# Order of matmuls in an attention-plus-MLP kernel: three constants of the order's planner against a table with one entry per group

## The chip, the cores and the metric

The kernel runs on one core of a Trainium2 chip. The metric is the time on the device of one execution, in microseconds (us); the median of several runs is given. Every detail of where the time goes comes from one execution that the hardware profiler recorded.

## The reference

Two steps in a row. The first is an attention with 32 inducing points over 4 batches of 12480 tokens of 128 channels; the second is an MLP of width 2048 with a leaky activation whose slope is a parameter.

```python
def mab(q, kv):
    s = scale * (q @ kv.transpose(0, 2, 1))
    s = s - s.max(-1, keepdims=True)
    a = np.exp(s)
    a /= a.sum(-1, keepdims=True) + 1e-09
    return a @ kv
h = mab(I, x)                 # x (4, 12480, 128), I: 32 inducing points per batch
attn = mab(x, h)              # (4, 12480, 128)

x = attn.reshape(49920, 128)
h = x @ w_in                  # (49920, 2048)
g = np.maximum(h, 0.0) + alpha * np.minimum(h, 0.0)
return g @ w_out              # (49920, 128), float32
```

## The kernel before

**The algebra.** The activation is written as alpha*h + (1 - alpha)*relu(h). The linear part is folded into one 128x128 matrix per batch. Since the attention's output for a token is a weighted mean of only 32 rows, the product with w_in is folded too: for each batch the 32 rows are multiplied by w_in once (`hW`), and a token's row of 2048 follows from its 32 weights, so this matmul contracts over 32 and takes only 32 of the array's 128 rows.

**The work of a group.** Tokens are taken in groups of 512 (the last one of a batch is smaller: 192). There are 25 groups per batch, 100 in all. For each group the kernel does

- 16 *fills* (`fill`): a matmul of 32 rows, `bank<-rep,hW`, which makes one chunk of 128 hidden channels for 512 tokens in a PSUM bank; ScalarE (ACT) or VectorE (DVE) takes it out of the bank through a relu into an SBUF tile `gt` (L608 and L611). The planner gives each to the engine that it expects to be done first.
- 16 x 4 *pieces* (`piece`): each chunk is contracted over its 128 channels with W1, in four matmuls of 32 rows each, `bank<-gt,W`, one on each of the array's four row tiles, all added up in the group's own accumulator bank.
- one *linear* term, `bank<-rep,hA`, which opens the accumulator.
- at the end (`finish`) a transpose on DVE (L658), a multiplication on GpSimd (POOL, L661) and four stores that POOL issues (L675).

There are 8 PSUM banks. The accumulators of groups in work and the banks between fill and relu share them.

**Lanes.** 92 of the 100 groups are *laned*; the others (two first, the small ones, two last) are done with full-array matmuls. A laned group starts on row tile 0 and does its 16 pieces there, moves to row tile 1 and does its 16 pieces there, and so on to row tile 3. So up to `LANES` = 4 groups are in work at once, one per row tile, and matmuls on different row tiles run side by side. At each move there is a fence: the pieces on the next row tile wait for the last one on the tile before. Fills can go to any row tile; one on a tile that has a lane takes a turn from that lane's pieces. At most `KEPT` - 1 = 65 chunks are kept in SBUF.

**What sets the order.** `tokens` builds the program once, ahead of the run. It keeps a planner's clock for each engine (`clk.pe`, `clk.act`, `clk.dve`, and for each bank the time it comes free) and in a loop writes the next matmul: it collects the candidates with the time at which each could go and a rank, and takes the earliest, by rank among equals. Candidates are pieces, lane entries, the start of a new group on row tile 0, and fills. PE, ACT and DVE run what was written in that order. Three choices in that loop matter here:

- *When a fill is due.* `hungry = min(clk.act, clk.dve) < clk.pe + HUNGRY` with `HUNGRY` = 600 (ns): when the engine that takes out relus and is done first has less than 600 ns of planned work ahead, a fill may go to any row tile and ranks ahead of a piece; otherwise it may go only to an empty row tile and ranks last.
- *When a new group may start.* `if f == 0 and queue and sum(map(bool, tile)) + len(moving) < LANES`: as soon as row tile 0 is free and fewer than four groups are in work.
- *Which row tile a fill takes.* Among equal times an empty one first (rank 0.5 against 0.6).

At the start of each laned group `run_tasks` also writes the work of that moment for attention: scores, exponentials, denominators, the loads of the next batch and its transposes. These hang on the number of the group, so their order against the groups is fixed, while their place among the matmuls follows the groups' starts.

Of the kernel before, what the change touches and what calls it, by code (L numbers as in the profile page):

```python
# [2 lines left out]

# [17 lines left out]
SUP = GRP * NQ  # L21
NBANK = 8
LANES = 4
HUNGRY = 600
TAIL = 2
AHEAD = 8
LAND = 8000
# [3 lines left out]
XTS = 8  # L31
DONE = 420
SWITCH = 110


@with_exitstack
def kernel(
# [23 lines left out]
    KC = DFF // P  # L61
# [47 lines left out]
    clk = Clock()  # L109
    idle = list(range(NBANK - 2))  # L110

    def bank():
        i = min(idle, key=lambda i: clk.free[i])
        idle.remove(i)
        clk.pe = max(clk.pe, clk.free[i])
        return banks[i]
# [12 lines left out]
    def mm(o, lhsT, rhs, start=True, stop=True, **kw):  # L129
        return pin(nc.tensor.matmul(o, lhsT, rhs, start=start, stop=stop, **kw))  # L130
# [454 lines left out]
    def spent(b, g, n):  # L585
        left[b, g] -= n
        if not left[b, g]:
            held.append((b, g))
# [26 lines left out]
    def piece(ch, i, rows=slice(0, P)):  # L615
        b, g, u = ch
        pp, nb, cp = shape_of(g)
        t = pp * nb
        return add(b, g, W1[rows, u * cp + i, :], seen[ch][0][rows, i * t : (i + 1) * t])

    def whole(ch):
        clk.pe = max(clk.pe, seen[ch][1])
        for i in range(shape_of(ch[1])[2]):
            piece(ch, i)
        clk.pe += 217
        spent(ch[0], ch[1], 4)
        seen.pop(ch)

    def linear(b, g, f):
        st = states[b]  # L630
        pp, nb, _ = shape_of(g)
        rows = slice(32 * f, 32 * f + 32)
        add(b, g, st.hA[rows, :], st.rep[g][rows, : pp * nb])
        spent(b, g, 1)

    def linear_whole(b, g):
        st = states[b]
        pp, nb, _ = shape_of(g)
        add(b, g, st.hAq[:], st.rep[g][:, : pp * nb])
        clk.pe += 217  # L640
        spent(b, g, 1)

    def flush():
        while held:
            finish(*held.pop(0))
# [166 lines left out]
    def tokens(st):  # L812
# [7 lines left out]
        laned = [y for y in every if y not in direct]  # L820
        first = {y: m for m, y in enumerate(laned)}
        wholes = [[] for _ in laned]
        for b in range(B - 1):
            c = first[b + 1, 0] - 1
# [28 lines left out]
        for b in range(B):  # L853
            base = T0 + (first[b, 0] if b else -2)
            for s in range(1, NS + 1):
                t = base + 4 * s - AHEAD if b or s > 2 else 4 * s - 2
# [48 lines left out]
        def run_tasks(t):  # L905
            for fn in tasks.pop(t, []):
                fn()
# [22 lines left out]

        clk.pe += SWITCH
        fence = ctx.enter_context(nc.semaphore())
        fenced = 0
        fences = {}
        queue = list(laned)
        tile = [None] * 4
        moving = []
        free_at = [clk.pe] * 4
        gate = {}
        closed = False  # L940
        fresh = {f: bank() for f in (2, 3)}

        def pause(t):
            return t in pauses or (t - T0 < len(wholes) and wholes[t - T0])

        def fillable():
            if not need or len(seen) >= KEPT - 1:
                return False
            b, g, _ = need[0]
            return b in states and g in states[b].rep and hasattr(states[b], "hW")  # L950

        while queue or moving or any(tile):
            best = []
            taken = {q for _, q, _ in moving}
            for f in range(4):
                if tile[f]:
                    y, todo = tile[f]
                    if todo[0] is None:
                        best.append((free_at[f], 0, f, "linear"))
                    elif (*y, todo[0]) in seen:  # L960
                        t = max(free_at[f], seen[*y, todo[0]][1] - 100)
                        best.append((t, 1, f, "piece"))
                else:
                    for y, q, t in moving:
                        if q == f:
                            best.append((max(free_at[f], t), 1, f, "enter"))
                    if f == 0 and queue and sum(map(bool, tile)) + len(moving) < LANES:
                        ch = (*queue[0], 0)
                        if ch in seen:
                            t = max(free_at[f], seen[ch][1] - 100 - SLOT)  # L970
                            best.append((t, 2, f, "start"))
            if fillable():
                since = max(min(clk.free[i] for i in idle) - 40, landed.get(need[0][:2], 0))
                hungry = min(clk.act, clk.dve) < clk.pe + HUNGRY
                for f in range(4):
                    t = max(free_at[f], since)
                    if hungry:
                        best.append((t, 0.5 + 0.1 * bool(tile[f]), f, "fill"))
                    elif not tile[f]:
                        best.append((t, 4 + (f in taken), f, "fill"))  # L980
            soon = min(max(x[0], clk.pe) for x in best) < clk.pe + 2 * SLOT
            for f in sorted(fresh):
                if soon and f not in taken:
                    best.append((free_at[f], 9, f, "warm"))
            assert best, (need[:2], len(seen), tile, moving, queue[:2])
            if closed:
                calm = [x for x in best if x[3] == "piece" and x[2] and x[2] not in gate]
                calm += [x for x in best if x[3] == "warm"]
                best = calm or [x for x in best if x[3] == "piece"] or best
            t, _, f, what = min(best, key=lambda x: (max(x[0], clk.pe), x[1]))  # L990
            closed = False
            clk.pe = max(clk.pe, t)
            rows = slice(32 * f, 32 * f + 32)
            if what == "start":
                m = first[queue[0]]
                if pause(T0 + m):
                    clk.pe = max(clk.pe, max(free_at) + SWITCH)
                    for ch in wholes[m]:
                        if ch[:2] not in begun:
                            linear_whole(*ch[:2])  # L1000
                        whole(ch)
                    flush()
                    run_tasks(T0 + m)
                    clk.pe += SWITCH
                    free_at = [clk.pe] * 4
                else:
                    run_tasks(T0 + m)
                tile[0] = [queue.pop(0), [None] + list(range(KC))]
                continue
            if what == "enter":  # L1010
                x = next(x for x in moving if x[1] == f)
                moving.remove(x)
                tile[f] = [x[0], list(range(KC))]
                gate[f] = fences[x[0], f]
                if f in fresh:
                    i = number[id(fresh.pop(f))]
                    clk.free[i] = clk.pe + SLOT
                    idle.append(i)
                continue
            if what == "warm":  # L1020
                mm(
                    fresh[f][:], W1[rows, 0, :],
                    W1[rows, 0:NB, :].rearrange("p k c -> p (k c)"), skip_group_check=True,
                )
                free_at[f] = clk.pe + SLOT
                continue
            if what == "fill":
                fill(need.pop(0), f)
            else:
                y, todo = tile[f]  # L1030
                u = todo.pop(0)
                if u is None:
                    linear(*y, f)
                else:
                    ch = (*y, u)
                    m = piece(ch, 0, rows)
                    if f in gate:
                        m._wait_ge(fence, gate.pop(f))
                    spent(*y, 1)
                    if f == 3:  # L1040
                        seen.pop(ch)
                    if not todo:
                        tile[f] = None
                        if f < 3:
                            pin(nc.tensor.drain(fusable=True)).then_inc(fence, 1)
                            fenced += 1
                            closed = True
                            fences[y, f + 1] = fenced
                            moving.append((y, f + 1, clk.pe + DONE))
                        flush()  # L1050
            free_at[f] = clk.pe + SLOT
        clk.pe = max(clk.pe, max(free_at) + SWITCH)
        for t in sorted(tasks):
# [12 lines left out]
        assert not tasks and not seen and not any(left.values()), (tasks, seen, left)  # L1066

    tokens(st)


# [28 lines left out]
```

## Time and profile before

| | us |
|---|---|
| median of 3 runs | 571.53 |
| lowest and highest | 570.17, 576.52 |
| the profiled execution | 570.76 |
| its span, first to last instruction | 569.0 |

| engine | busy us | share of the span |
|---|---|---|
| PE (matmuls) | 551.0 | 97% |
| DVE | 500.3 | 88% |
| ACT | 510.4 | 90% |
| POOL | 408.5 | 72% |

Busy time is the union of an engine's records, so two matmuls side by side on different row tiles count once, and records of ACT or DVE that overlap by their pipeline count once. A row of the list of groups names the line of the kernel, engine and operation, the tiles written and read, the shape, the count, and then busy us, mean ns of one, and the idle time before them with what ended it. L130 is the line of the helper that records nearly all matmuls, so those are told apart by their tiles: `gt,W` are pieces, `rep,hW` fills, `rep,hA` linear terms, `W` alone are dummy matmuls on lanes that are still empty at the beginning.

The mean granted clock of TensorE over the span is 0.992.

### The profile page before, as it was taken

What the parts mean: (1) busy time and instruction counts of PE and PEld (TensorE: products, weight loads), DVE (VectorE), ACT (ScalarE), POOL (GpSimd) and SP (SyncE); (2) the same over time, 40 slices, a digit from 0 to 9 for tenths busy, and PEclk for the clock granted to TensorE, in tenths of its full rate; (3) what the DMA queues carried; (4) which work ended last, traced back from release to release, by engine and by line L of the source; (5) the groups of instructions that cost most, each with busy time, mean ns of one, the idle gap of its engine ahead of it and who ended that gap; (6) DMA issues with size and microseconds to landing.
All of it is one profiled execution on the core that took longest, in us unless ns stands there. A gap on an engine that the chain in (4) does not pass through costs nothing.

```text
span 569.0 us, 21411 instructions
## 1 busy us (share of the span) xinstructions
PE 551.0 (97%) x8862; PEld 306.7 (54%) x8866; DVE 500.3 (88%) x856; ACT 510.4 (90%) x1010; POOL 408.5 (72%) x600
## 2 busy tenths in 40 slices
PE   4999999999999999999999999999999999999995
PEld 4645555555555555555555555655555555555542
DVE  3689898989989999999989999999989999999961
ACT  2479999998989999999999999999999999999960
POOL 6646567777799788787879976766768677777761
PEclk9999999999999999999999999999999999999988
DMA  9976997746888989586785965324424234423223
GB/s 196 226 136 124 150 206 143 144 90 118 163 163 140 170 154 156 134 138 133 122 151 124 168 134 126 83 64 102 98 57 109 57 95 107 105 61 56 53 57 58
DMA packets 111201, 69.25 MB, mean 122 GB/s; under 512 B 79824, under 2 KB 101696, under 8 KB 111104
## 3 DMA queue, kind: packets, MB, share of 16 engines
q0 software_dynamic: 23280, 38.53, 36.0%
q1 hardware_dynamic: 85152, 28.52, 25.6%
q8 instruction: 69, 1.13, 0.8%
q10 hardware_dynamic: 2672, 0.84, 0.6%
q14 instruction: 28, 0.23, 0.2%
HBM read 41.00 MB, written 28.95 MB: 123 GB/s over the span
## 4 chain that ended last, share of the span: by engine, by line
PE 83%; issue 4%; POOL 3%; ACT 3%; DVE 3%; DMA 2%; SPq 0%; POOLq 0%; DVEq 0%
PE bank L130 81%; ACT gt L608 3%; POOL out_dram L675 2%; PE bank L218 2%; DVE gt L611 1%; POOL ob L661 1%; DMA ind_f<-in_inducing_dram 1%; DMA rt<-rd 1%; DVE hW L305 1%; DMA rdT<-rt 0%; DVE ot L658 0%; DMA out_dram<-ob 0%; DVE xT L224 0%; DVE xn L776 0%; SPq L675 0%
## 5 line engine op out<-in xcount | busy, mean ns | idle before, releaser
L130 PE MATMUL bank<-gt,W 32*128 32x512 bf16 (+1 forms) x6013 | 493.9, 374 | 0.8 <-issue 0.4
L608 ACT ACTIVATE gt<-bank 128x512 bf16<-128x512 f32 x925 | 475.5, 608 | 15.9 <-PE bank L130 11.7
L611 DVE TENSOR_SCALAR gt<-bank 128x512 bf16<-128x512 f32 x643 | 408.6, 679 | 29.9 <-PE bank L130 23.5
L130 PE MATMUL bank<-rep,hW 32*128 32x512 bf16 (+1 forms) x1600 | 415.3, 369 | 0.9 <-DVE hW L305 0.3
L130 PEld LDWEIGHTS <-W 32*128 32x128 bf16 (+1 forms) x6081 | 231.8, 92 | 167.0 <-issue 89.0
L675 POOL DMA_DIRECT2D out_dram<-ob x384 | 246.1, 670 | 39.0 <-POOL ob L661 27.9
L661 POOL TENSOR_TENSOR ob<-ot,rdT 128x512 f32<-128x512 f32 (+1 forms) x100 | 108.8, 1089 | 103.5 <-DVE ot L658 92.2
L130 PEld LDWEIGHTS <-hW 32*128 32x128 bf16 x1600 | 130.2, 91 | 46.0 <-issue 23.6
L658 DVE STREAM_TRANSPOSE ot<-bank 128x512 f32<-128x512 f32 (+1 forms) x100 | 69.5, 694 | 15.1 <-PE bank L130 14.6
L172 POOL DMA_DIRECT2D xn<-in_x_dram x70 | 40.0, 644 | 5.1 <-DMA xn<-in_x_dram 2.4
L130 PE MATMUL bank<-rep,hA 32*128 32x512 bf16 x94 | 35.1, 377 | 0.5 <-DVE hW L305 0.3
L224 DVE COPY xT<-bank 128x1024 bf16<-128x1024 bf16 (+1 forms) x16 | 10.7, 672 | 5.4 <-PE bank L218 5.1
L245 ACT ACTIVATE e1t<-bank 128x256 bf16<-128x256 f32 (+1 forms) x13 | 4.8, 371 | 10.4 <-PE bank L130 10.3
L130 PEld LDWEIGHTS <-hA 32*128 32x128 bf16 x94 | 8.5, 91 | 7.1 <-issue 5.2
L218 PE MATMUL bank<-ident,xn 128*128 128x128 bf16 x128 | 11.3, 242 | 0.9 <-DVE xn L776 0.9
L130 PE MATMUL bank<-W 32*128 32x512 bf16 x65 | 11.4, 376 | 0.0
L130 PE MATMUL bank<-xT,hT 128*32 128x512 bf16 (+1 forms) x98 | 10.4, 389 | 0.4 <-ACT gt L608 0.4
L493 ACT ACTIVATE e<-bank,rs 128x512 bf16<-128x512 f32 x12 | 8.5, 707 | 2.6 <-PE bank L130 2.5
L218 PEld LDWEIGHTS <-xn 128*128 128x128 bf16 x128 | 8.7, 109 | 2.1 <-DVE xn L776 1.0
L130 PE MATMUL bank<-IT,xT 128*128 128x32 bf16 x192 | 8.0, 179 | 1.0 <-issue 0.8
L493 ACT ACTIVATE e<-bank 128x512 bf16<-128x512 f32 x12 | 7.3, 609 | 1.8 <-PE bank L130 1.5
L130 PEld LDWEIGHTS <-e 128*128 128x128 bf16 x96 | 4.3, 96 | 7.6 <-issue 7.5
(100 smaller groups left out, 145.7 us busy)
## 6 DMA issues: line engine op xcount, KB each, us to landing
out_dram<-ob POOLq DMA_DIRECT2D x372, 64.0 KB, 3.0
rep<-e2d SPq DMA_DIRECT2D x92, 128.0 KB, 2.9
xn<-in_x_dram POOLq DMA_DIRECT2D x48, 128.0 KB, 5.2
xn<-in_x_dram POOLq DMA_DIRECT2D x22, 256.0 KB, 7.4
e2d<-e SPq DMA_DIRECT2D x24, 128.0 KB, 2.9
rdT<-rt SPq DMA_DIRECT2D x96, 8.0 KB, 2.4
w_out_f<-in_moe_w_out_dram POOLq DMA_DIRECT2D x4, 256.0 KB, 11.2
xs<-in_x_dram SPq DMA_DIRECT2D x1, 512.0 KB, 4.8
```

The source lines that it names most:

```text
L130: return pin(nc.tensor.matmul(o, lhsT, rhs, start=start, stop=stop, **kw))
L172: pin(nc.gpsimd.dma_start(out=xn[:, i * w : (i + 1) * w, :], in_=src[:, i * w : (i + 1) * w, :]))
L218: pin(nc.tensor.transpose(tp[:, k * P : (k + 1) * P], xn[:, q, j * C : (j + 1) * C], ident[:]))
L224: pin(nc.vector.tensor_copy(out=dst, in_=tp[:, :w]))
L245: pin(nc.scalar.activation(out=e1t[:pp, :nb, :].rearrange("p k m -> p (k m)"), in_=ps[:pp, : nb * M], func=EXP, scale=scale,))
L305: pin(nc.vector.tensor_scalar(out=out, in0=in_, scalar1=st.rs[:, 0:1], scalar2=1.0 / scale, op0=MULT, op1=MULT,))
L493: pin(nc.scalar.activation(out=e2[:].rearrange("p (t j i) -> p t j i", j=n, i=32), in_=turned(ps[:pp, :w], n), func=EXP, scale=scale_of(st ...
L608: pin(nc.scalar.activation(out=gt[:, :w], in_=ps[:, :w], func=RELU))
L611: pin(nc.vector.tensor_relu(gt[:, :w], ps[:, :w]))
L658: pin(nc.vector.transpose(out=ot[:, :t], in_=acc[:, :t]))
L661: pin(nc.gpsimd.tensor_tensor(out=ob[:, :t].rearrange("p (k m c) -> p k m c", k=nb, c=32), in0=ot[:, :t].rearrange("p (k m c) -> p k m c", ...
L675: pin(eng.dma_start(out=dst[a], in_=ob[32 * a : 32 * a + 32, :t].rearrange("p (b k) -> p b k", k=32),))
```

## The change

The three choices get a value per laned group. `KNOBS` lists 40 triples (threshold, room, penalty): threshold 300, 450, 600, 800 or 1100 ns in place of `HUNGRY`; room 16, 10, 6 or 3; penalty 0 or 60 ns. `PLAN` has one letter, an index into `KNOBS`, for each of the 92 laned groups. When the loop first chooses to start group m, it sets the triple of that group, and goes round once more with it, so the start itself is already judged by the new values.

- The threshold is used as before.
- A room below 16 limits the fourth lane: with three groups in work, a new one starts only when the group on row tile 3 has at most that many pieces left.
- A penalty of 60 adds 60 ns to the time of a fill on a row tile that has a lane, when candidates are compared.

The triple of the kernel before is (600, 16, 0); 11 of the 92 entries are this one. 57 have a lower threshold, 16 a higher one, 30 have a room below 16, 25 have the penalty.

```diff
-HUNGRY = 600
...
+KNOBS = [(h, r, c) for h in (300, 450, 600, 800, 1100) for r in (16, 10, 6, 3) for c in (0, 60)]
+PLAN = (
+    "yqbyysrquizoaHqiuiiiobNbizFqbhjiFawqweqiyqiiDbqy"
+    "iqqimNqihauihaFicikaebaoaaxiaFbgahiiiaDakiki"
+)
...
+        hungry_at, room, cost = 600, KC, 0
+        plans = list(PLAN)
+        assert len(plans) == len(laned)
...
-                    if f == 0 and queue and sum(map(bool, tile)) + len(moving) < LANES:
+                    lanes = sum(map(bool, tile)) + len(moving)
+                    if f == 0 and queue and lanes < LANES and (
+                        lanes < LANES - 1 or room == KC or tile[3] and len(tile[3][1]) <= room
+                    ):
...
-                hungry = min(clk.act, clk.dve) < clk.pe + HUNGRY
+                hungry = min(clk.act, clk.dve) < clk.pe + hungry_at
...
-                        best.append((t, 0.5 + 0.1 * bool(tile[f]), f, "fill"))
+                        best.append((t, 0.5 + 0.1 * bool(tile[f]), f, "fill", cost if tile[f] else 0))
...
-            t, _, f, what = min(best, key=lambda x: (max(x[0], clk.pe), x[1]))
+            t, _, f, what, *_ = min(best, key=lambda x: (max(x[0], clk.pe) + sum(x[4:]), x[1]))
+            if what == "start" and plans:
+                m = first[queue[0]]
+                if len(laned) - len(plans) == m:
+                    hungry_at, room, cost = KNOBS[string.ascii_letters.index(plans.pop(0))]
+                    continue
```

More of the change, by code (lines that the diff above doesn't have):

```diff
@@ L1 @@
 import math
+import string
 from contextlib import ExitStack
```

## The prediction

> **What bounds the kernel now.** I read the page first, then the busy time by stretch, then the timeline. The page:
>
> ```profile
> span 569.0 us, 21411 instructions
> PE 551.0 (97%) x8862; PEld 306.7 (54%) x8866; DVE 500.3 (88%) x856; ACT 510.4 (90%) x1010; POOL 408.5 (72%) x600
> PE   4999999999999999999999999999999999999995
> DVE  3689898989989999999989999999989999999961
> ACT  2479999998989999999999999999999999999960
> PEclk9999999999999999999999999999999999999988
> ...
> L130 PE MATMUL bank<-gt,W 32*128 32x512 bf16 (+1 forms) x6013 | 493.9, 374 | 0.8 <-issue 0.4
> L608 ACT ACTIVATE gt<-bank 128x512 bf16<-128x512 f32 x925 | 475.5, 608 | 15.9 <-PE bank L130 11.7
> L611 DVE TENSOR_SCALAR gt<-bank 128x512 bf16<-128x512 f32 x643 | 408.6, 679 | 29.9 <-PE bank L130 23.5
> L130 PE MATMUL bank<-rep,hW 32*128 32x512 bf16 (+1 forms) x1600 | 415.3, 369 | 0.9 <-DVE hW L305 0.3
> ```
>
> PE, ACT and DVE look full from 60 us to the end, and the clock is not held back before the tail. But "97%" is the union of up to four matmuls at a time. The timeline shows the true pace:
>
> ```profile
> 45.70 0.37 PE L130 MATMUL bank<-gt,W 32*128 32x512 bf16 x1
> ...
> 45.92 0.37 PE L130 MATMUL bank<-gt,W 32*128 32x512 bf16 x1
> 46.04 0.38 PE L130 MATMUL bank<-W 32*128 32x512 bf16 x2
> 46.09 0.38 PE L130 MATMUL bank<-rep,hW 32*128 32x512 bf16 x1
> 46.13 0.37 PE L130 MATMUL bank<-gt,W 32*128 32x512 bf16 x1
> 46.25 0.38 PE L130 MATMUL bank<-W 32*128 32x512 bf16 x2
> 46.35 0.37 PE L130 MATMUL bank<-gt,W 32*128 32x512 bf16 x1
> ```
>
> The pieces here are all on row tile 0. They start 0.22, 0.21, 0.22 us apart, so a row tile takes a new 512-column matmul each 0.217 us, though a record lasts 0.374. The program has 7623 matmuls of 32 rows after the first lane start; on four row tiles they need 7623/4 x 0.217 = 413.5 us at least. The lane stretch lasts from 42 to 550 us, 508. Full-array matmuls among them (721, by their starts 44 ns to the next matmul on average: 32 us) leave 508 - 413.5 - 32, about 62 us in which row tiles stand empty although PE shows as busy. The evictors are no fuller:
>
> ```profile
> 60.00:550.00 490.00, 488.29 (x8079) 271.37 (x8071) 455.10 (x770) 473.38 (x940) 369.07 (x522) 1.00 0.61 118
> ```
>
> ```profile
> 301.07 19.03 ACT L608 ACTIVATE gt<-bank 128x512 bf16<-128x512 f32 x38
> 239.56 2.45 DVE L611 TENSOR_SCALAR gt<-bank 128x512 bf16<-128x512 f32 x4
> ```
>
> Columns of the first line: stretch, length, then busy time and count of PE, PEld, DVE, ACT, POOL. The runs without a pause give the real pitch: (19.03 - 0.608)/37 = 0.498 us on ACT, (2.45 - 0.679)/3 = 0.590 on DVE. ACT's 940 instructions at 0.498 are 468 of 490 us, so some 22 us are free; DVE's 593 relus of the stretch at 0.590 are 350, its other 177 instructions at most as long each, 104: 454, so at least 36 are free. No engine is a hard bound; they hold each other up.
>
> **Where PE waits.** I laid the matmul starts of the trace beside the program's order and took for each lane matmul the time by which it starts later than both its predecessor in the order and its row tile's last start + 0.214 us. Above 25 ns each, this gives: first pieces of a chunk, waiting for their relu, 16.1 us (the first reader of each gt, 1472 of them); fills waiting for the eviction of an earlier fill in the same bank, 19.0 us; fence waits at lane changes, 11.2 us; linear terms, which wait for a bank to accumulate in, 11.6 us; full-array work, 10.1 us.
>
> **The change, part by part.** The number of fills, pieces, relus and DMAs stays; SP's instructions have the same order, POOL's differ only in where a group's store stands against loads and others. Of the 92 laned groups 11 keep the old three values, 57 get a lower threshold, 16 a higher one, 30 a limit on the fourth lane, 25 the penalty. Two dummy matmuls fewer and five relus from ACT to DVE: 5 x 0.498 against 5 x 0.590, nothing while both have over 20 us free, and at most 3 us if DVE had none. What moves is the order:
>
> (1) Distance from a chunk's fill to its first piece, counted in matmuls of the order. The median is 28 before and 76 after, since three lanes in place of four leave a row tile to the fills. Wait by distance, from the trace of before, and the counts:
>
> - under 18: 71 ns each, 45 before, 9 after: 3.2 us becomes 0.6
> - 18 or 19: 46 ns, 124 to 8: 5.7 becomes 0.4
> - 20 or 21: 34 ns, 147 to 12: 5.0 becomes 0.4
> - 22 or 23: 8 ns, 144 to 17: 1.2 becomes 0.1
> - 24 and more: 1 ns, 1012 to 1426: 1.0 becomes 1.4
>
> Sum 16.1 becomes 2.9: **-13.2 us**. The end at the other side is 0, all of it coming back elsewhere (below).
>
> (2) Distance between two fills into one bank. Fewer lanes hold fewer accumulators, so it goes up: at 22 and more 596 before, 843 after; below 20, 342 before and 252 after. At the mean wait of each distance over the whole trace, 19.0 would become 16.0, -3.0. But where pieces wait, the evictors catch up and fills wait less, so these prices are too kind to a kernel without piece waits. The laned groups 32 to 43 and 56 to 67 (counted from 0) have few piece waits; at their prices (45 ns at 18 or 19, 13 at 20 or 21, 7 at 22 or 23, 18 at 24 or 25) the new distances cost 20.9: +2.0. I take **+2.0**, the stretches that are like the new state, and keep -3.0 and +2.0 as the ends.
>
> (3) Linear terms and full-array matmuls waiting for a bank: 351 ns a group in the stretches with few piece waits, 180 in groups 22 to 31 and 46 to 55. If the 41 groups with many piece waits (these and 70 to 90) all rose by 170 ns, this is 7 us; at least 0. The former groups also carry other work in these waits, so I take **+3**.
>
> (4) Collisions. Cutting the order into rounds that use no row tile twice gives 2049 rounds before and 2028 after: 21 x 0.217 = 4.6 us at most. The least is 0, since a busy row tile need not hold up the next matmul: in the timeline above the order is dummies on tiles 2 and 3 (started 46.25), then the fill on tile 1, which started at 46.09, ahead of them. I take half, **-2.3**.
>
> The Trainium skill, "TensorE: Matmul & The Clock Gate", section "Step-by-step: what each phase is for", says that matmuls stay in program order and only weight loads are pulled ahead. By that rule a collision holds everything and the whole 4.6 counts, sum -12.8; by the row above, which does not agree for different row tiles, it would be 0 and the sum -8.2.
>
> Fences are as many, 3 x 92: no change. Stores on POOL: 1.09 + 4 x 0.67 = 3.8 us a group, and groups now end at 3.3 to 7 us from each other; a pair at 3.3 makes POOL late by 0.5 us, which three ob buffers hide; without them DVE's next transpose would wait that 0.5 us.
>
> Sum: -13.2 + 2.0 + 3.0 - 2.3 = -10.5. The profiled execution took 570.8 us (span 569.0 and 1.8 around it), so 560.3; the median of the runs, 571.5, is 0.8 higher, so **561** as a median.
>
> **Rivals.** A: the waits come back at the banks. Where a piece no longer waits, the next fill does, because the evictors take as long as before. For it: a group took 5.25 us in 22 to 31 (lane matmuls 4.28 of it) and 5.35 in 32 to 43 (4.39), so 0.97 and 0.96 beyond them, though the piece waits are 0.36 and 0.06. Saved per group 0.01, times 92 about 1 us: 570.5. Against it: ACT has 22 us free, and the new order spaces the fills better (688 of them 4 matmuls apart, 363 before; 167 within 2 of the last, 265 before). The Trainium skill, "TensorEngine Tiling (Array Packing)", section "PSUM Bottleneck", has this rule: tiling speeds up TensorE but not the eviction of PSUM, which may then bound. The 468 of 490 us on ACT agree in part.
>
> B: the decoupling works fully, (1), (2) and (4) at their best and nothing in (3): -13.2 - 3.0 - 4.6 = -20.8, 550.7 by the median. For it the same spacing; against it, ACT would be left without any pause.
>
> C, slower: the evictors run dry. In 57 groups a fill is now due only when an evictor has less than 300 or 450 ns of planned work left, under one relu (608). ACT and DVE then wait for PE at L608 and L611, now 11.7 + 23.5 = 35.2 us. Each engine's wait has to grow by 10.5, 21 in sum, to eat the gain; that is where it decides. Doubled, it is 17.6 per engine: -10.5 + 17.6 = +7.1, 578.6. Against it: 16 groups go up, and with the fills evenly placed few gaps are long.
>
> That the change does nothing is out: the distances differ.
>
> **Numbers.** Forecast 0.6, A 0.2, B 0.1, C 0.1. A change under 1% (5.7 us) is about what a measurement cannot tell from none. Faster: forecast and B, 0.7; same: A, 0.2; slower: C, 0.1. The range takes in B at its lower end, 550, and A at its upper, 571; C is left out.
>
> **What would show it.** Right: rows of ACT and DVE relus busy a larger share of the stretch 60 to 550, and that stretch ending about 10 us earlier; piece waits near 3 us, fill waits near 21. (1) is wrong if piece waits stay above 8; A is right if fill waits pass 30; C if the idle behind L608 and L611 "PE bank L130" grows past 56 us in sum. The whole is wrong if the tail after the last lane, 549.7 to 569, changes by more than 2 us, since nothing in it is edited.

## The result, and the profile after

Over 20 runs of each kernel the median went from 568.91 to 566.00 us, 2.9 less. The ratio that is used from here on compares undisturbed runs alone and leaves out as slow six of the changed kernel's 20 runs (570.99 to 575.81 us) and one of before (576.52). It is 0.9927, 95% interval 0.9901 to 0.9953: 4.2 us faster, between 2.7 and 5.6. A second measurement of the unedited changed kernel (10 runs) gave 0.9985, 0.9945 to 1.0024, which alone can't be told from no change; a gain of about half a per cent lies in both intervals. The forecast was 10.5 less, so the sign was right and the size more than twice what came.

The first profile of the changed kernel has a stop of 3.3 us in it, which lasts only 1.0 us in the second measurement, `again` (told at the end). So the profile read here is that of `again`, whose execution took 565.5 us. Its page:

```profile
span 563.7 us, 21364 instructions
PE 543.9 (96%) x8864; PEld 294.8 (52%) x8864; DVE 499.7 (89%) x861; ACT 504.6 (90%) x1005; POOL 408.9 (73%) x600
...
L135 PE MATMUL bank<-gt,W 32*128 32x512 bf16 (+1 forms) x6016 | 488.8, 374 | 1.3 <-issue 1.0
L613 ACT ACTIVATE gt<-bank 128x512 bf16<-128x512 f32 (+1 forms) x920 | 469.5, 616 | 19.3 <-PE bank L135 15.2
L616 DVE TENSOR_SCALAR gt<-bank 128x512 bf16<-128x512 f32 (+1 forms) x648 | 406.1, 676 | 21.8 <-PE bank L135 17.7
```

The two evictors' waits for PE at the relus are 15.2 + 17.7 = 32.9 us, 35.2 before: hardly less. How the order has changed is seen in the timeline of PE at 202 us, first of the changed kernel, then of the one before (start, length, then the instructions merged):

```profile
202.04 0.38 PE L135 MATMUL bank<-gt,W 32*128 32x512 bf16 x3
202.05 0.37 PE L135 MATMUL bank<-rep,hW 32*128 32x512 bf16 x1
202.26 0.38 PE L135 MATMUL bank<-gt,W 32*128 32x512 bf16 x3
202.27 0.37 PE L135 MATMUL bank<-rep,hW 32*128 32x512 bf16 x1
202.47 0.38 PE L135 MATMUL bank<-gt,W 32*128 32x512 bf16 x3
202.48 0.37 PE L135 MATMUL bank<-rep,hW 32*128 32x512 bf16 x1
```

```profile
201.95 0.38 PE L130 MATMUL bank<-rep,hW 32*128 32x512 bf16 x1
201.95 0.80 PE L130 MATMUL bank<-gt,W 32*128 32x512 bf16 x6
202.41 0.37 PE L130 MATMUL bank<-rep,hW 32*128 32x512 bf16 x1
202.42 0.37 PE L130 MATMUL bank<-gt,W 32*128 32x512 bf16 x1
202.57 0.37 PE L130 MATMUL bank<-rep,hW 32*128 32x512 bf16 x1
202.59 0.59 PE L130 MATMUL bank<-gt,W 32*128 32x512 bf16 x4
```

Where three lanes run, the changed kernel goes in even steps: three pieces and a fill, one on each row tile, each 0.21 to 0.22 us. Before, fills came 0.46 and 0.16 us apart. How much work both did in the same 480 us, before and then after:

```profile
60.00:540.00 480.00, 478.52 (x7968) 266.40 (x7963) 446.27 (x756) 464.04 (x921) 361.74 (x512) 1.00 0.62 119
```

```profile
60.00:540.00 480.00, 475.98 (x8010) 257.00 (x8005) 448.63 (x765) 461.27 (x922) 363.70 (x514) 1.00 0.64 119
```

42 more matmuls (first count) and, on DVE and ACT (third and fourth), 10 more instructions: half a per cent on PE.

The waits of PE, taken as in the prediction but from the first lane start to the last lane's end alone (so 18.8 where it had 19.0), in us, with those of two experiments below. Each wait counts with what it has above 25 ns:

| | before | changed | half relus, order before | half relus, order after |
|---|---|---|---|---|
| lane stretch | 507.6 | 504.4 | 492.7 | 495.5 |
| first piece for its relu | 16.1 | 2.3 | 10.0 | 3.7 |
| fill for the last one in its bank | 18.8 | 36.8 | 5.8 | 9.9 |
| fences | 11.2 | 11.4 | 15.8 | 17.7 |
| linear terms for a bank | 11.6 | 11.0 | 8.4 | 8.7 |
| full-array work | 10.3 | 8.2 | 9.3 | 8.1 |

The piece waits went as forecast. The fills wait 18 us more. By the prediction's own way of adding up, that is where the expected gain went. The first-piece waits of the last two columns are uncertain: they depend on which record is laid beside which matmul of the order, and other ways to lay them give 1.3 to 4.6 in place of 10.0 and 1.3 to 3.1 in place of 3.7. Nothing below rests on them.

### The profile page after: what moved, and what is told of

Read it like the earlier page. It is cut to its first block, busy times and chain, and to the rows that moved or that the text cites. A ratio compares the mean times of both kernels' runs of the same rounds, so it can differ in the third digit from the quotient of the medians.

```text
span 569.2 us, 21360 instructions
## 1 busy us (share of the span) xinstructions
PE 546.6 (96%) x8860; PEld 295.4 (52%) x8864; DVE 500.4 (88%) x861; ACT 505.3 (89%) x1005; POOL 408.7 (72%) x600
## 4 chain that ended last, share of the span: by engine, by line
POOL 35%; PE 32%; issue 20%; PEld 5%; DVE 4%; DMA 2%; POOLq 0%; SPq 0%; PEldq 0%; ACT 0%; DVEq 0%
PE bank L135 30%; POOL out_dram L680 23%; POOL ob L666 11%; PEld L135 5%; DVE gt L616 2%; PE bank L223 2%; POOL xn L177 1%; DMA ind_f<-in_inducing_dram 1%; DMA rep<-e2d 1%; DVE ot L663 1%; DVE hW L310 1%; DMA out_dram<-ob 0%; DVE xT L229 0%; POOLq L666 0%; PEldq L1061 0%
## 5 line engine op out<-in xcount | busy, mean ns | idle before, releaser
L135 PE MATMUL bank<-gt,W 32*128 32x512 bf16 (+2 forms) x6013 | 490.7, 376 | 4.3 <-issue 3.6
L613 ACT ACTIVATE gt<-bank 128x512 bf16<-128x512 f32 (+1 forms) x920 | 470.2, 615 | 23.9 <-PE bank L135 19.6
L616 DVE TENSOR_SCALAR gt<-bank 128x512 bf16<-128x512 f32 (+1 forms) x648 | 406.6, 677 | 26.8 <-PE bank L135 22.7
L135 PEld LDWEIGHTS <-W 32*128 32x128 bf16 (+1 forms) x6079 | 228.9, 92 | 188.5 <-issue 114.6
L135 PEld LDWEIGHTS <-hW 32*128 32x128 bf16 x1600 | 134.0, 92 | 36.7 <-issue 18.6
L135 PE MATMUL bank<-W 32*128 32x512 bf16 x63 | 10.3, 376 | 0.0
```

The lines of the kernel that those rows point to most:

```text
L613: pin(nc.scalar.activation(out=gt[:, :w], in_=ps[:, :w], func=RELU))
L616: pin(nc.vector.tensor_relu(gt[:, :w], ps[:, :w]))
```

## The experiments

All ratios are to the kernel before, run on the same chip, with a 95% interval. Theory 1: the evictors set the pace, and PE waits for them in one form or another. Theory 2: PE's own order sets it, above all collisions on row tiles, 21 fewer after. Theories 3 and 4 came after the first eight runs. Theory 3: a lane stretch is what the row tiles need alone, plus about 0.55 of PE's waits, which only change their place (by the numbers below it was 0.63 before and 0.56 in the changed kernel). Theory 4: the longer distances feed the evictors better, and that is the gain. "What the row tiles need alone" is an estimate, worked out from the order, two measured numbers and an assumption: each row tile takes a matmul each 0.2165 us, full-array matmuls take 44 ns, and, which no run shows, one more matmul may stand ready behind the one that a row tile works on. In the trace of before it can be more: the first fill of the lanes starts at 42.29 us, ahead of three pieces on row tile 0 (42.49, 42.71 and 42.93) that stand before it in the order. The estimate gives 459.0 for before, 458.3 for the changed order.

**The changed kernel once more** (`again`, no edit).

> The changed kernel once more, unedited, for a second profile. In the first one all engines stood still for 3.3 us at 88.4 us. Without such a pause the span should be about 562 us; waits of first pieces for their relu 1.5 to 3 us in sum, as in the first profile, and waits of fills for a bank 45 to 60 us, where before had 35.7.

The span is 563.7, 1.7 above the one expected; piece waits 2.3; fill waits 36.8, and 46.1 with those of a first fill in a bank (9.3). The 35.7 that the expectation names for before is not in the table's measure: by that, all waits of before are 76.7 and the rows of the table 68.0, so its fill waits, those of first fills among them, are 27.5 at most.

**Evictors with half the columns** (`relu_half_before`, `relu_half_after`). The order of the matmuls is unchanged. The edit, in both orders:

```diff
-            pin(nc.scalar.activation(out=gt[:, :w], in_=ps[:, :w], func=RELU))
+            n = w // 2 if cp == 1 else w
+            pin(nc.scalar.activation(out=gt[:, :n], in_=ps[:, :n], func=RELU))
...
+            rhs = bass.AP(tensor=rhs.tensor, offset=rhs.offset, ap=[rhs.ap[0], [0, 2], [1, t // 2]])
```

> The order of before; each relu takes out only the first 256 of the 512 columns of a chunk, and the pieces read these twice, so PE does the same work and ACT and DVE little more than half (the second half of the tokens is not computed). Theory 1, the evictors set the pace and PE waits for them in one form or the other: the waits for relus and for banks go, some 35 of them and part of the linear and full-array ones, 530 to 540 us. Theory 2, PE's own order sets the pace (collisions on row tiles and fences): little changes, 555 to 568 us.

> The same with the order of after. Theory 1: with fast evictors the two orders differ only by what PE does by itself, and the new order's longer distances are worth nothing: within 3 us of the run with the order of before, either way. Theory 2: the 21 rounds saved remain, 4 to 5 us faster than that run.

Measured 0.9801 (0.974 to 0.9862) and 0.9775 (0.971 to 0.984). These rows of the page of the run with the order of before show that the evictors' relus became shorter (608 to 386 ns on ACT, 679 to 424 on DVE) and the evictors stood idle much of the time:

```profile
PE 532.4 (97%) x8866; PEld 302.6 (55%) x8866; DVE 369.8 (67%) x856; ACT 372.2 (68%) x1010; POOL 409.5 (75%) x600
...
L609 ACT ACTIVATE gt<-bank 128x256 bf16<-128x256 f32 x925 | 334.8, 386 | 128.1 <-PE bank L130 106.1
L613 DVE TENSOR_SCALAR gt<-bank 128x256 bf16<-128x256 f32 x643 | 270.1, 424 | 129.5 <-PE bank L130 117.4
```

They wait for PE for 106.1 + 117.4 us, and still only 2% are gained, 11 us where Theory 1 wanted 28 or more: PE has its own bound at a lane stretch of some 493 or a little less. That speaks for Theory 2. But the 4 to 5 us between the two orders that it asked for were not there: 0.9775/0.9801 = 0.997, and with the ends of the intervals 0.985 to 1.010, so the two orders are not told apart, as Theory 1 had it for this pair. The waits of fills fell from 36.8 to 9.9 in the new order, so those waits are for the evictors.

**Three lanes** (`lanes3`: `LANES = 3`).

> The kernel before with three lanes in place of four and nothing else. The median distance from a fill to its first piece is 147 matmuls (28 before, 76 after), distances below 20 between fills into one bank 213 (342 before, 252 after), but 2106 rounds without a repeated row tile (2049 before, 2028 after). Theory 1: as much gained from the distances as by the change, 562 to 568. Theory 2: 57 rounds more at 0.217 are +12, 578 to 584.

Measured 1.0326 (1.0275 to 1.0377), 18 us slower, past both. Long distances don't bring a gain by themselves. The row tiles alone would need 10 us more (469.3), and the evictors ran short of fills:

```profile
L608 ACT ACTIVATE gt<-bank 128x512 bf16<-128x512 f32 x927 | 465.7, 633 | 36.3 <-PE bank L130 34.9
L611 DVE TENSOR_SCALAR gt<-bank 128x512 bf16<-128x512 f32 (+1 forms) x641 | 401.5, 681 | 54.1 <-PE bank L130 51.0
```

85.9 us of waiting for PE, 35.2 before.

**60 collisions more, the same order** (`tiles_worst`). `MOVED` lists 60 fills and the row tile of the matmul ahead of each.

```diff
     def fill(ch, f):
+        f = MOVED.get(len(calls), f)
+        calls.append(f)
```

> The kernel before with its order of matmuls unchanged, except that 60 of the fills go to the row tile of the matmul just ahead of them. That makes 2109 rounds without a repeated row tile in place of 2049; all distances between fill, first piece and next fill into the bank stay as they were. Theory 2 (collisions on row tiles cost a whole round each): 60 x 0.217 = +13.0, 580 to 583. Theory 1 (the waits between PE and the evictors set the pace, and a busy row tile lets the next matmul pass): 567 to 571.

Measured 1.0106 (1.0055 to 1.0157): +6.0, or 3.1 to 8.9. Between the two, so 0.10 us for each collision (0.05 to 0.15), about half a round. At this price the 21 rounds of the change would be worth 2.1 us.

**Fewer collisions without a table** (`rounds_450`, `rounds_600`; the first also has `HUNGRY = 450`).

```diff
-            t, _, f, what = min(best, key=lambda x: (max(x[0], clk.pe), x[1]))
+            t, _, f, what = min(best, key=lambda x: (max(x[0], clk.pe) + (217 if x[3] in ("fill", "piece", "linear") and x[2] in used else 0), x[1]))
...
+                if f in used:
+                    used.clear()
+                used.add(f)
```

> The kernel before without a table: threshold 450 for all groups, and a fill, piece or linear term on a row tile that was used since the last repeat is put back by 217 ns when candidates are compared. 2004 rounds (2049 before, 2028 after), but short distances: median 24 from fill to first piece, 557 chunks under 22 (316 before, 29 after), 540 fills under 20 from the last one into their bank (342 before, 252 after). Theory 2: 45 rounds x 0.217 = -9.8, 557 to 561. Theory 1: waits for relus and banks as long as before or longer, 569 to 578.

> The same with the threshold of before, 600. 2014 rounds and long distances: median 109 from fill to first piece, 13 chunks under 22; 368 fills under 20 into their bank. Theory 2: 35 x 0.217 = -7.6, 559 to 563. Theory 1: piece waits go and fill waits come in their place, as in the changed kernel, 564 to 568.

Measured 1.0547 (1.05 to 1.0593) and 1.0241 (1.0191 to 1.0291): 31 and 14 us slower, past both theories each time. Theory 2 falls: the count of rounds alone says nothing. In `rounds_450` piece waits were 33.9 and fill waits 35.6 (first fills in a bank counted in), both high, which Theory 1 gives the direction of but not the size. What held these two back so far was not settled.

**One part of the table alone** (`thr_only`, `room_only`, `no_room`). The edit is which of the three values is taken, for the first:

```diff
-                    hungry_at, room, cost = KNOBS[string.ascii_letters.index(plans.pop(0))]
+                    hungry_at, _, _ = KNOBS[string.ascii_letters.index(plans.pop(0))]
```

> The thresholds of the table alone; room and penalty as before (16, 0). 2077 rounds; median distance 24, 547 chunks under 22. Theory 2: 28 x 0.217 = +6.1, 573 to 577. Theory 1: piece waits a little above those of before, 569 to 573.

> The rooms of the table alone (limit on the fourth lane); threshold 600 and penalty 0 as before. Distances as in the changed kernel: median 104 from fill to first piece, 35 chunks under 22, 269 fills under 20 into their bank. But 2073 rounds (2049 before, 2028 after); row tiles alone, without a wait, would need 4.4 us more than before. Theory 3, a lane stretch is what the row tiles need alone plus some 0.55 of the waits, and the waits only change their place: 569 to 575. Theory 4, longer distances are what brought the gain: 563 to 567.

> The rest of the table: thresholds and penalties, without the rooms. Distances short (median 21, 746 chunks under 22), 2095 rounds; row tiles alone 7.1 us more than before. Theory 3: +7 and the longer piece waits, 576 to 583. Theory 4: piece waits above those of before, 570 to 578. If the parts of the table add up, this and the run with the rooms alone together make the change's -4.

Measured 1.0156 (1.0109 to 1.0202), 1.0118 (1.007 to 1.0166) and 1.0393 (1.0351 to 1.0436): 9, 7 and 22 us slower. `thr_only` and `no_room` (medians 579.75 and 591.71) are past both theories. The six runs of `room_only` lie between 572.47 and 582.37; their median, 579.76, is 11 us above before's 568.37. Rooms alone and the rest without rooms would add up to +29; together they are -4. The parts don't add. Each value moves every later choice of the planner, so the letters make one order as a whole; it has fewer collisions (2028 rounds) than the orders of the parts (2077, 2073 and 2095). But few collisions and long distances together don't make the gain either: `rounds_600` has 2014 rounds and a median distance of 109, better than the changed kernel in both, and is 14 us slower than before. It has more short distances into a bank (368 fills under 20, against 252); whether these are the cause was not tried. `room_only` has nearly the distances of the changed kernel and is slower than before, so Theory 4 in its plain form, that distances are the gain, falls too; the 569 to 575 of Theory 3 is met at its edge by the ratio (575.1) and missed by the median of all its runs.

**Pieces with half the columns** (`piece_half_before`, `piece_half_after`). The order is unchanged again.

```diff
-        return add(b, g, W1[rows, u * cp + i, :], seen[ch][0][rows, i * t : (i + 1) * t])
+        n = t // 2 if cp == 1 else t
+        return add(b, g, W1[rows, u * cp + i, :], seen[ch][0][rows, i * t : i * t + n], n)
```

> The order of before; each piece multiplies only the first 256 of the 512 tokens of its chunk (the others lack the nonlinear part), so PE has a little over half of its work and the evictors all of theirs. Theory 3: the evictors are left as the bound; ACT and DVE need 468 and 454 of 490 by their pitch, so the lane stretch falls from 508 to 470 to 490, and with the shorter tail the whole is 525 to 550. If PE's order alone set the pace, it would fall by over 100.

> The same with the order of after. Theory 3: within 4 us of the run with the order of before, since both have the same relus; what the change gains comes from how PE and the evictors mesh, which is gone when PE has time to spare. Theory 4: the new order feeds the evictors better, and gains more here than with full pieces, 6 us or more.

Measured 0.9767 (0.9728 to 0.9806), 555.55 us, and 0.9599 (0.955 to 0.9649), 544.53. Between them 0.9828, by the ends of the intervals 0.974 to 0.992: the new order is 9.8 us faster (4 to 15) when PE has time to spare. That is the second part of Theory 4, against Theory 3, whose 525 to 550 for the order of before was missed as well. The rows of the two pages, before's order and then after's:

```profile
L608 ACT ACTIVATE gt<-bank 128x512 bf16<-128x512 f32 x925 | 470.6, 615 | 10.4 <-PE bank L130 9.0
L611 DVE TENSOR_SCALAR gt<-bank 128x512 bf16<-128x512 f32 x643 | 403.2, 676 | 26.2 <-PE bank L130 21.8
```

```profile
L613 ACT ACTIVATE gt<-bank 128x512 bf16<-128x512 f32 (+1 forms) x920 | 463.3, 628 | 10.7 <-PE bank L135 8.9
L616 DVE TENSOR_SCALAR gt<-bank 128x512 bf16<-128x512 f32 (+1 forms) x648 | 401.5, 674 | 15.4 <-PE bank L135 11.4
```

DVE's wait for PE falls from 21.8 to 11.4, ACT's stays. The fall is as large as the 9.8; that it is the cause was not shown. And PE with little over half of the work gained only 13 us in the order of before: the evictors, fed in these orders, are a bound too, at a lane stretch of 498 there and of 487 with the new order. Theory 3 had put it at 470 to 490.

## Why the prediction was right or wrong

The sign was right, and 566.0 lies between the 561 of the forecast and the 570.5 of rival A, in a range that was wide enough to hold both. Part of the 5 us to the forecast's median is chance in the start: 571.5 was the median of three runs of before, and 20 gave 568.9. The gain of 4.2 is nearer to A's 1 than to the forecast's 10.5.

The two pairs with lighter work on one side give the picture. With half the columns in each relu, both orders end at a lane stretch of 493 to 496; with half the columns in each piece, at 498 and 487; with both whole, at 508 and 504. So PE and the evictors are each within some 4% of the end. The new order takes about 10 us off where PE has time to spare. That this is the size of the forecast is chance, since the forecast added up waits of PE. Where the evictors have time to spare, it gains nothing that could be measured, though up to some 8 us are not ruled out by the intervals. With both whole, 4 arrive.

Step by step:

- **(1) piece waits, -13.2.** Right: 16.1 became 2.3, -13.8. The counts by distance carried over.
- **(2) fill waits, +2.0.** This is the step that failed: 18.8 became 36.8, +18. The term took the price of each distance from groups of before that were thought to be like the new state: 45, 13, 7 and 18 ns at 18 or 19, 20 or 21, 22 or 23, 24 or 25 matmuls. In `again` it was 55, 18, 27 and 19, and still 19 at 26 and more; most of what was missed is at 22 or 23, where 430 fills are. The bound of -3.0 to +2.0 for this term was too narrow by a factor of nine on its upper side. What the traces show in its place is that the evictors run later behind the fills: on the mean a relu starts 0.55 us after its fill in before and 0.58 in `again`, and ends 1.19 and 1.22 after it, so banks come free some 35 ns later. The matmuls in between pass no faster, short distances apart: at 22 or 23 matmuls the next fill's turn comes 1.28 us after the last fill in before and 1.31 in `again`, at 18 or 19 1.14 and 1.10. Why the evictors run later stays open; the prediction had said that they catch up where pieces wait, and priced it too low.
- **(3) linear terms and full-array work, +3.** Wrong in sign, little in size: 11.6 and 10.3 became 11.0 and 8.2, -2.7.
- **(4) collisions, -2.3.** Not contradicted, and not shown. The half was a choice between 0 and 4.6. At the 0.10 us that `tiles_worst` shows, 21 are -2.1; the estimate for the row tiles alone goes from 459.0 to 458.3, -0.7; and the pair with half relus shows no gain that could be measured. A collision that holds everything would have cost 13.0 us in `tiles_worst`; 6.0 were measured. The Trainium skill, "TensorE: Matmul & The Clock Gate", section "Step-by-step: what each phase is for", says that matmuls stay in program order and only weight loads are pulled ahead. Between row tiles this run does not agree in full.
- **Fences and the tail.** Right: 11.2 and 11.4. From the lane stretch's end to the span's, 19.3 became 17.6, inside the 2 us named, and for a cause told below.
- **The sum.** Waits were added up as if each lay on the path. With the measured sizes the same sum gives -13.8 + 18.0 - 2.7 - 2.1 = -0.6, next to nothing, so that a gain came after all is not what this way of adding up says: here the right sign is luck. All waits of the lane stretch, those of first fills in a bank among them, went from 76.7 to 81.6 while the stretch became 3.2 shorter, in place of the 10 that the prediction named as a sign of being right. Row tiles still work off what stands ready while PE waits: by the estimate above the stretch is 507.6 - 459.0 = 48.6 over what the row tiles need alone, for 76.7 of waits, and 46.1 for 81.6 after. A wait of a fill may cost less than one of a piece, but the cost of each kind was not measured apart.

Of the rivals, A ("the waits come back at the banks") is what happened in mechanism, by the mark set for it, fill waits past 30; its time, 570.5, missed the gain that was left. `piece_half_before` gains only 13 us from nearly half of PE's work, and `relu_half_before` shows PE as near to its own bound. The Trainium skill, "TensorEngine Tiling (Array Packing)", section "PSUM Bottleneck", says that eviction may bound once matmuls are tiled. The first of the two runs agrees. C is out: the evictors' waits for PE fell to 32.9 instead of passing 56. B is out by the time.

What the 4.2 are made of stays open. Fewer collisions are worth 0.7 to 2.1 by the two estimates above. The rest may be the better feed of the evictors that `piece_half_after` shows, as far as PE lets it through; the two were not separated in the full kernel.

## What to carry to other kernels

When two sides of a pipeline are each within a few per cent of the end, a wait that is removed on one is to be priced by what the other side can still give, not by its length; halve the load of one side at a time to learn both bounds before pricing an order. Prices by distance in instructions hold only while the engine on the other side keeps the same lag; here it grew by some 35 ns, and the waits doubled. Three settings that steer a greedy planner don't add up: the whole table was 4 us faster and its parts alone 7 to 22 us slower, so a part taken from it has to be measured as its own order.

## What the runs showed of the hardware that was not expected

A matmul on a busy row tile lets the next one on another tile go first, as in the timeline at 46.09 us; forced collisions cost 0.10 of their 0.217 us.

The first profile of the changed kernel shows PE stopped from 88.7 to 91.9 us, and ACT and DVE, which ran out of work, from 89.3 on; PE waited for no semaphore there. In `again` PE stops at the same matmuls, for 1.0 us; in before no stop inside the lanes is longer than 0.6. From the first profile's timeline of PE, then that of `again`, then the first profile's busy time by stretch (PE, PEld, DVE, ACT and POOL, granted clock, share of DMA, GB/s):

```profile
88.24 0.43 PE L135 MATMUL bank<-gt,W 32*128 32x512 bf16 x2
91.93 0.61 PE L135 MATMUL bank<-gt,W 32*128 32x512 bf16 x2 [3.26 <-issue]
```

```profile
89.60 0.39 PE L135 MATMUL bank<-gt,W 32*128 32x512 bf16 x2 [1.03 <-issue]
```

```profile
90.00:92.00 2.00, 0.07 (x4) 0.07 (x7) 0.00 (x0) 0.00 (x0) 0.62 (x1) 0.73 1.17 284
92.00:98.00 6.00, 6.00 (x59) 2.92 (x61) 2.69 (x4) 3.18 (x6) 2.25 (x3) 0.52 0.85 183
98.00:104.00 6.00, 6.00 (x123) 2.96 (x116) 5.68 (x10) 5.41 (x11) 3.75 (x7) 1.00 0.22 46
```

From the stop on the clock stood at about half until 98 us, and in the last 6 of them PE did 59 matmuls, against 123 in the next 6. Stop and half clock are about the 5.5 us by which that execution was longer than `again`.

The traces say what PE lacked. Instructions come by DMA too, and one of the instruction queues moves 69 packets of 16 KB in each trace, one for each 257 instructions of PE. In before such a packet landed at 85.9 us, in `again` at 88.3, in the first profile at 90.5, in `no_room` at 91.7; PE went on at 89.6, 91.9 and 93.6 in the last three, after stops of 1.0, 3.3 and 5.5 us. All stops of PE over 0.6 us inside the lanes, twelve in these traces and those of `room_only`, `rounds_600`, the two with half relus and `piece_half_before`, end 1.3 to 1.9 us after a packet of this queue landed. So PE had most likely run out of instructions. The DMA engines were full in the stop shown (284 GB/s), but whether that made the packet late was not tried.

How often the changed kernel has a long stop is not known, since only two of its executions were profiled. The granted clock speaks for more than one: it was 0.988 in the execution with the 3.3 us, 0.985 to 0.988 in nine of the 30 runs of the changed kernel (this one among them), and never below 0.991 in the 36 executions of before for which it is on record.

The end of the lanes brings the same half clock, for 6.8 us in before, 3.4 in `again` and 10.2 in `room_only`. In before it held over both of these stretches, in `again` over the first alone:

```profile
549.30:552.70 3.40, 3.18 (x8) 0.96 (x8) 0.72 (x1) 0.05 (x1) 3.32 (x5) 0.50 0.38 77
552.70:556.10 3.40, 3.40 (x9) 1.21 (x8) 0.00 (x0) 0.00 (x0) 0.00 (x0) 0.50 0.33 58
```

```profile
546.60:550.00 3.40, 3.40 (x9) 1.18 (x8) 0.72 (x1) 0.00 (x0) 2.89 (x4) 0.50 0.37 77
550.00:553.40 3.40, 3.40 (x17) 1.56 (x16) 0.72 (x1) 0.00 (x0) 0.51 (x1) 1.00 0.45 77
```

3.4 us more at half clock are 1.7 us of full clock, as much as the tail's 19.3 against 17.6. A difference of two single profiles of this kernel under 2 us can be this alone.
